# Attention and a gated feed-forward layer on one core: the weights' low parts move to VectorE, four ticks decode twice, and the second unit's input is normalised a tick sooner

## The chip, the core and the metric

The kernel runs on one core of a Trainium2 chip. Its time is the device time of one execution in microseconds (us); lower is better. The engines are PE (TensorE, matrix products), DVE (VectorE), ACT (ScalarE) and POOL (GpSimd), each working through a queue of its own in order; SP (SyncE) issues the loads and stores. PE's granted clock has two levels, 1.2 and 2.4 GHz, shown as a share of the higher one.

## The reference, cut to what matters

Windowed attention over 8 x 8 heads of 576 positions (heads 0 to 3: the last 32 keys; heads 4 to 7: every fourth key of the last 128), then a root-mean-square norm and a gated feed-forward layer on 4608 tokens of width 512, with 1536 hidden columns:

```python
scores = where(mask, q @ k.T / 8, -1e9)
attn = softmax(scores) ; x = attn @ v
xn = x / sqrt(mean(x * x) + 1e-6) * rms_g
g = xn @ w_gate
val = xn @ w_val
out = (g * sigmoid(g) * val) @ w_out
```

The weights reach the kernel as 64-bit numbers.

## The kernel before, in words

The tokens are worked on in 16 units of 288. For each unit the feed-forward layer runs over 12 blocks j of 128 hidden columns in three ticks each: the gate product g, the value product v, and the output product acc of block j - 1. The counter of ticks over the whole main loop is `t` (L793): unit 0 begins at t = 2, unit 1 at t = 36. In the same ticks PE does the attention of the next unit: scores s, transposed probabilities t, outputs o (`products`, L450). Their ticks are a table, `q_at` (L767 for unit 1), that `plan` (L745) turns into events; `plan` also sets when the unit's sum of squares is formed ("sum", PE's rps) and when its norm is applied ("apply", PE's bps, `rms_apply`, L567).

What the other engines do in a tick is put off with `later(dt, rank, fn)` and issued by `flush` (L113) in order of rank. So the order on each engine's queue is fixed by tick and rank. From rank 0 up, a tick issues on DVE the product h of tanh and value (`prod`, L677), the scores' maxima (`scores_max`, L354), the tanh product (`silu`, L664), a decoding step (rank 5) and the low part of a weight (rank 6).

- **Decoding.** The weights come in 18 pairs of 1 MB, `raw`, three buffers. A pair is rescaled by ACT (`rebase`, L151, from pair 3 on), its sign word is cleared by POOL (L162), and DVE puts the number together in two steps from pair 4 on (`rest`, L176, and `whole`, L180; three before that). The step `whole` frees the buffer and issues the next load. `decode(1)` (L797) issues one step per tick in unit 0; the last pair, 17, is whole at t = 32. For the last pair, the rescaling and the clearing are issued right with its first step. Once no more than two steps are left, a second pool of buffers opens (L800), from which unit 1's x gets parts of its space.
- **Splitting.** Unit 0 multiplies with the decoded 32-bit weights. From unit 1 on each weight stands as a high and a low part (`split_weight`, L227): ACT casts the high part, then DVE or POOL subtracts it, which gives the low part lo (L243). The 36 weights are split in the order of their use in unit 0: at even ticks from 4 to 30 on DVE, and from tick 37 on in every tick, on DVE in odd and on POOL in even ones. The line that sets this:

```python
if used and (t >= SPLITS[2] or t % 2 == 0 and SPLITS[0] <= t < SPLITS[1]):
    later(0, 6, lambda: split_weight(*used.pop(0), V if t < SPLITS[1] or t % 2 else G))
```

- **The norm.** PE's rps sums the squares at tick 27; DVE adds the constant, POOL takes the power and splits the root (L537 to L543), a tick later DVE and ACT spread it over a matrix rd (`spread`, L546), and PE's bps multiplies that with ones at tick 30. In the ticks after that DVE scales x (L585) and ACT, DVE and POOL split it.

PSUM has few banks: the gate product of j + 1 takes the bank of the value product of j, and one bank, s, holds every score from tick 4 on.

Of the kernel before, what the change touches and what calls it, by code (L numbers as in the profile page):

```python
# [14 lines left out]
ALU = mybir.AluOpType  # L15
# [22 lines left out]
REBASES = 5, 9, 17, 23  # L38
BUSY = 7, 3
SIGNS = 4  # L40
SPLITS = 4, 31, 37


ORDER = [(0, 0, "q"), (0, 1, "q"), (0, 0, "v"), (0, 2, "q"), (0, 0, "w"), (0, 1, "v"), (0, 3, "qv"), (0, 2, "v"),
         (0, 0, "g"), (0, 0, "w"), (0, 0, "w"), (1, 0, "qv")]
# [22 lines left out]
def attn_moe(ctx: ExitStack, tc: tile.TileContext, qk_in, v_in, w_gate, w_val, w_out, rms_g, outT):  # L68
# [4 lines left out]
    V, A, G, PE = nc.vector, nc.scalar, nc.gpsimd, nc.tensor  # L73
# [36 lines left out]
    def later(dt, rank, fn):  # L110
        put_off.setdefault(now[0] + dt, []).append((rank, fn))

    def flush():  # L113
        for _, fn in sorted(put_off.pop(now[0], []), key=lambda e: e[0]):
            fn()
# [11 lines left out]
    wts, raws, fs, his, los, used = {}, {}, {}, {}, {}, []  # L127
# [74 lines left out]
    def decode(k):  # L202

        for i in range(k):
            later(0, 5 + 2 * i, step)
        later(0, 8.9, rebase_next)
# [16 lines left out]
    def single(kind, j):  # L223
        n = pieces.index((kind, j))
        return fs[n // 2][:, n % 2]

    def split_weight(kind, j, e):  # L227
        n = pieces.index((kind, j))
        m, k = divmod(n, 2)

        tag = f"hi{n if n % 4 == 3 and n < 2 * NP - 4 else n - n % 4}"
        if tag not in his:
            parts = 1 if n % 4 == 3 and n < 2 * NP - 4 else 3 if n < 2 * NP - 4 else 4
            his[tag] = cst.tile([P, parts, NC, P], F32R, tag=tag, name=f"{tag}_{kind}{j}")
        hi = his[tag][:, 0 if tag == f"hi{n}" else n % 4]
        if k == 0:
            los[m] = cst.tile([P, 2, NC, P], F32R, tag=f"slot{state['free']}", name=f"lo_{m}")
        else:
            state["free"] = m
        lo = los[m][:, k]  # L240
        wts[kind, j] = hi, lo
        A.copy(out=hi, in_=single(kind, j))
        e.tensor_tensor(out=lo, in0=single(kind, j), in1=hi, op=ALU.subtract)  # L243


    heads, vs, late = {}, {}, []
# [188 lines left out]
    def bursts(u):  # L435
        return [(u, c, i) for c in range(NC) for i in range(len(geometry(u, c)[0]))]
# [197 lines left out]
    def bank(kind, j):  # L634
        return "gv"[(j + (kind == "v")) % 2]
# [12 lines left out]
    def gate(u, j):  # L648
        g_ps = group("g", u, j)
        if u == 0:  # L650
            used.append(("g", j))
        g = g_ps[:, :U]

        def tanh():
            nonlocal g
            t = (sb.tile([P, U], F32, tag="hhi", name=f"h_{j}", bufs=2) if u == 0 else
                 sb.tile([P, U], F32, tag="th", name=f"th_{u}_{j}", bufs=1))
            if u + j == 0:
                g = sb.tile([P, U], F32, tag="hhi", name="g_first", bufs=2)
                V.tensor_tensor(out=g, in0=g_ps[:, :U], in1=root[0], op=ALU.mult)  # L660
            A.activation(out=t, in_=g, func=AF.Tanh, scale=0.5)  # L661
            gv[u, j] = t

        def silu():  # L664
            t = gv[u, j]
            V.scalar_tensor_tensor(out=t, in0=t, scalar=1.0, in1=g, op0=ALU.add, op1=ALU.mult)  # L666

        later(1, 0 if u + j else 0.65, tanh)
        later(1, 0.8, silu)
        return g_ps[:, U:U + 2 * QB]  # L670

    def val(u, j):
        v_ps = group("v", u, j)
        if u == 0:
            used.append(("v", j))

        def prod():  # L677
            t = gv[u, j]
            V.tensor_tensor(out=t, in0=t, in1=v_ps[:, :U], op=ALU.mult)  # L679
            if u + j == 0:  # L680
                V.tensor_tensor(out=t, in0=t, in1=root[0], op=ALU.mult)

        def parts():
            t = gv.pop((u, j))
            if u == 0:
                hs[u, j] = t
                return
            hi = sb.tile([P, U], F32R, tag="hhi", name=f"hhi_{u}_{j}", bufs=2)
            lo = late[0].tile([P, U], F32R, tag="hlo", name=f"hlo_{u}_{j}", bufs=2)
            A.copy(out=hi, in_=t)  # L690
            G.tensor_tensor(out=lo, in0=t, in1=hi, op=ALU.subtract)  # L691
            hs[u, j] = (hi, lo)

        later(1 if u + j else 2, 0, prod)
        later(1 if u + j else 2, 0.5, parts)
        return v_ps[:, U:U + 2 * QB]

    def proj(u, j):
        if u == 0:
            used.append(("o", j))  # L700
        h = hs.pop((u, j))
        for d in range(NC):
            if j == 0:
                acc[u, d] = ps.tile([P, 512], F32, tag=f"acc{d}", name=f"acc_{u}_{d}")[:, :U]
            three(acc[u, d], weight("o", u, j), d, h, j == 0, j == NJ - 1)
            if j == NJ - 1:
                later(1, 0.7, lambda d=d: give(u, d))
# [35 lines left out]
    events = {}  # L743

    def plan(u, base, q_at, t_at, o_at):  # L745
        for b, *ts in zip(bursts(u), q_at, t_at, o_at):
            for kind, t in zip("qto", ts):
                events.setdefault(base + t, {})[kind] = b
        events.setdefault(base + o_at[-1] + (4 if u == 1 else 3), {})["sum"] = u
        events.setdefault(base + o_at[-1] + (4, 7, 5)[min(u, 2)], {})["apply"] = u  # L750

    def attend(t_ps, **tags):
        e = events.pop(now[0], {})
        if any(k in e for k in "qto"):
            products(e.get("q"), e.get("t"), e.get("o"), t_ps, **tags)
        if "sum" in e:
            rms_sum(e["sum"])
        if "apply" in e:
            rms_apply(e["apply"])

    ends = nb + LAG + OUT + 5
    plan(0, 0, range(nb), range(LAG, nb + LAG), range(LAG + OUT, nb + LAG + OUT))
    for u in range(1, NU):
        q_at = [LAST - (LAST - EARLY[u > NNAT]) * (nb - 1 - k) // (nb - 1) for k in range(nb)]
        t_at, o_at = [t + 5 for t in q_at], [t + 8 for t in q_at]
        if u < NNAT:
            q_at = (-4, -2, -1, 1, 2, 4, 5, 7, 8, 10, 11, 13, 14, 16)  # L767
            t_at, o_at = [t + 5 for t in q_at], [t + 7 for t in q_at]
        plan(u, ends - 2 + 3 * NJ * (u - 1), q_at, t_at, o_at)
    for n in range(ends):  # L770
# [19 lines left out]
    for u in range(NU):  # L790
        for j in range(NJ):
            for part in range(0 if u + j else 2, 3):
                t = 3 * (u * NJ + j) + part  # L793
                if used and (t >= SPLITS[2] or t % 2 == 0 and SPLITS[0] <= t < SPLITS[1]):
                    later(0, 6, lambda: split_weight(*used.pop(0), V if t < SPLITS[1] or t % 2 else G))
                if u == 0:
                    decode(1)  # L797
                opening = len(ops) <= 2
                flush()
                if opening and not late:  # L800
                    early.close()
                    late.append(ctx.enter_context(tc.tile_pool(name="late", bufs=2)))
                if part == 0:
                    free = gate(u, j)
                elif part == 1:
                    free = val(u, j)
                else:
                    if prev is not None:
                        proj(*prev)
                    prev = (u, j)  # L810
                    free = None
                    if "t" in events.get(now[0], {}):
                        free = ps.tile([P, 512], F32, tag=bank("g", j), name=f"t_{u}_{j}")[:, :2 * QB]
                attend(free, s_tag="acc2" if t < 4 else "s")
                now[0] += 1
# [70 lines left out]
```

## Time and profile before

| | us |
|---|---|
| median of 3 runs (1146.93 to 1150.12) | 1148.58 |
| the profiled execution | 1148.22 |
| its span, first to last instruction | 1146.4 |
| PE busy in the span | 1120.8 (98%) |
| DVE busy | 793.4 (69%) |
| ACT busy | 714.6 (62%) |
| POOL busy | 620.8 (54%) |

The chain that ended last lies on PE for 85% of the span and on DVE for 6%. The mean granted clock is 0.997. An engine's busy time is the time in which it executes; what it waits for stands in brackets behind an instruction in the timeline, with the engine and line that ended the wait.

### The profile page before, as it was taken

To read this page: it belongs to the slowest core of one execution; us is meant where nothing else is said; L and a number is where in the kernel's file an instruction comes from. 1 tells how busy PE (TensorE), PEld (TensorE's weight loads), DVE (VectorE), ACT (ScalarE), POOL (GpSimd) and SP (SyncE) were. 2 spreads that over 40 slices of the span, in tenths; PEclk is the share of its full clock that TensorE was granted. 3 is DMA by queue.
4 is the path that set the end of the run, shared out by engine and by line. 5 is a ranking of instruction groups with operands and counts; after the bars stand their busy time and mean duration, and the time that the engine had idled before them with its cause. 6 is when DMAs were issued, how large, how long until landed. Compare 5 with 4: busy or idle time off the path is not lost.

```text
span 1146.4 us, 25956 instructions
## 1 busy us (share of the span) xinstructions
PE 1120.8 (98%) x8357; PEld 1088.0 (95%) x8357; DVE 793.4 (69%) x2893; ACT 714.6 (62%) x2610; POOL 620.8 (54%) x1073
## 2 busy tenths in 40 slices
PE   8898888999999999999999999999999999999998
PEld 7676778999999999999999999999999999999998
DVE  7889865867767586776758677585866758586411
ACT  5686676766657576675757657576765757576311
POOL 8235576655546465564547556465655646565211
PEclk9999999999999999999999999999999999999999
DMA  9555211311212121121212213121221312120000
GB/s 246 168 202 205 89 48 38 93 50 50 83 38 82 40 84 52 52 89 33 79 41 83 58 41 94 34 86 41 71 63 45 95 27 87 41 79 15 2 21 21
DMA packets 61545, 82.19 MB, mean 72 GB/s; under 512 B 7298, under 2 KB 41090, under 8 KB 61410
## 3 DMA queue, kind: packets, MB, share of 16 engines
q1 hardware_dynamic: 61410, 80.54, 23.6%
q8 instruction: 67, 1.10, 0.4%
q14 instruction: 68, 0.56, 0.2%
HBM read 71.08 MB, written 9.44 MB: 70 GB/s over the span
## 4 chain that ended last, share of the span: by engine, by line
PE 85%; DVE 6%; ACT 4%; issue 2%; DMA 1%; POOL 1%; POOLq 0%; SPq 0%; DVEq 0%; ACTq 0%
PE acc L622 8%; PE g L622 8%; PE v L622 8%; PE acc L623 8%; PE g L624 8%; PE g L623 8%; PE acc L624 8%; PE v L623 8%; PE v L624 8%; PE s L489 3%; PE o L477 3%; PE o L478 1%; PE busy L739 1%; ACT t L376 1%; DVE lo L243 1%
## 5 line engine op out<-in xcount | busy, mean ns | idle before, releaser
L691 POOL TENSOR_TENSOR hlo<-th,hhi 128x288 fp32r<-128x288 f32 x180 | 145.2, 807 | 201.5 <-ACT hhi L690 153.7
L624 PE MATMUL acc<-hhi,lo 128*128 128x288 f32 x720 | 212.2, 295 | 0.0
L391 POOL TENSOR_SCALAR t<-t,sum 72x72 f32<-72x72 f32 (+3 forms) x414 | 154.0, 384 | 71.9 <-DVE sum L386 65.2
L624 PE MATMUL v<-xhi,lo 128*128 128x288 f32 x612 | 180.8, 295 | 0.0
L624 PE MATMUL g<-xhi,lo 128*128 128x288 f32 x612 | 180.6, 295 | 0.0
L376 ACT ACTIVATE t<-t,sum 96x128 f32<-96x128 f32 (+3 forms) x448 | 165.6, 375 | 11.7 <-DVE sum L366 11.0
L690 ACT CAST hhi<-th 128x288 fp32r<-128x288 f32 x180 | 78.1, 434 | 141.0 <-DVE th L679 138.8
L305 POOL TENSOR_TENSOR vlo<-vt,vhi 128x128 fp32r<-128x128 f32 x196 | 93.3, 476 | 109.3 <-ACT vhi L301 96.9
L421 DVE TENSOR_TENSOR xraw<-o,xraw 64x96 f32<-64x96 f32 (+1 forms) x392 | 106.8, 272 | 56.4 <-ACT xraw L411 50.4
L661 ACT ACTIVATE th<-g 128x288 f32<-128x288 f32 x180 | 73.9, 410 | 106.6 <-PE g L624 87.7
L624 PEld LDWEIGHTS acc<-hhi,lo 128*128 128x128 f32 x720 | 135.6, 188 | 0.0
L666 DVE SCALAR_TENSOR_TENSOR th<-th,g 128x288 f32<-128x288 f32 x180 | 80.4, 447 | 69.4 <-ACT th L661 69.4
L624 PEld LDWEIGHTS v<-xhi,lo 128*128 128x128 f32 x612 | 115.3, 188 | 0.0
L624 PEld LDWEIGHTS g<-xhi,lo 128*128 128x128 f32 x612 | 115.0, 188 | 0.0
L622 PE MATMUL g<-xhi,hi_g 128*128 128x288 f32 x357 | 110.7, 310 | 1.6 <-DVE sum L385 0.9
L335 POOL TENSOR_TENSOR ks<-qk,ks 128x288 fp32r<-128x288 f32 (+2 forms) x112 | 111.0, 1005 | 0.0
L622 PE MATMUL acc<-hhi,hi_o 128*128 128x288 f32 x360 | 110.8, 308 | 0.0
L411 ACT COPY xraw<-o 64x96 f32<-64x96 f32 (+1 forms) x392 | 101.5, 259 | 12.5 <-PE o L478 10.1
L679 DVE TENSOR_TENSOR th<-th,v 128x288 f32<-128x288 f32 x180 | 81.5, 453 | 38.1 <-PE v L624 30.0
L623 PE MATMUL acc<-hlo,hi_o 128*128 128x288 f32 x360 | 106.9, 297 | 0.0
L361 DVE TENSOR_TENSOR t<-s,mask 96x256 f32<-96x256 f32 (+3 forms) x196 | 71.5, 365 | 50.9 <-PE s L489 45.7
L623 PE MATMUL g<-xlo,hi_g 128*128 128x288 f32 x322 | 94.8, 294 | 0.0
(184 smaller groups left out, 3581.2 us busy)
## 6 DMA issues: line engine op xcount, KB each, us to landing
qk<-in_qk_dram SPq DMA_DIRECT2D x60, 288.0 KB, 2.8
vt<-in_v_dram SPq DMA_DIRECT2D x196, 64.0 KB, 1.9
qk<-in_qk_dram SPq DMA_DIRECT2D x30, 352.0 KB, 3.0
out_dram<-ot SPq DMA_DIRECT2D x64, 144.0 KB, 1.9
qk<-in_qk_dram SPq DMA_DIRECT2D x30, 304.0 KB, 2.8
raw<-in_w_gate_dram SPq DMA_DIRECT2D x12, 512.0 KB, 4.7
raw<-in_w_val_dram SPq DMA_DIRECT2D x12, 512.0 KB, 5.3
raw<-in_w_out_dram SPq DMA_DIRECT2D x12, 512.0 KB, 4.3
```

Of the source, the lines that this page charges most:

```text
L305: G.tensor_tensor(out=vl, in0=vs.pop(b), in1=vh, op=ALU.subtract)
L335: ek.tensor_tensor(out=ks[:, 1, :nkt], in0=kr, in1=ks[:, 0, :nkt], op=ALU.subtract)
L376: A.activation(out=t[:nq, a, :n], in_=t[:nq, a, :n], func=AF.Exp, scale=-1.0, bias=sm[:nq, a, 0:1], accum_out=sm[:nq, a, 1:2] if u else None)
L391: (V if u == 0 and (c, i) > (NC - 1, 0) else G).tensor_scalar(out=t[:nq, a, :n], in0=t[:nq, a, :n], scalar1=sm[:nq, a, 3:4], scalar2=1.0, ...
L411: A.copy(out=to[a * D:(a + 1) * D], in_=o[a * D:(a + 1) * D, (2 + a) * nq:(3 + a) * nq])
L421: V.tensor_tensor(out=to[rows], in0=o[rows, a * nq:(a + 1) * nq], in1=to[rows], op=ALU.add)
L622: PE.matmul(out, wh[:, cc, :], xh, start=start, stop=False)
L623: PE.matmul(out, wh[:, cc, :], xl, start=False, stop=False)
L624: PE.matmul(out, wl[:, cc, :], xh, start=False, stop=stop)
L666: V.scalar_tensor_tensor(out=t, in0=t, scalar=1.0, in1=g, op0=ALU.add, op1=ALU.mult)
L679: V.tensor_tensor(out=t, in0=t, in1=v_ps[:, :U], op=ALU.mult)
L691: G.tensor_tensor(out=lo, in0=t, in1=hi, op=ALU.subtract)
```

## The change

Four things change in the table of ticks, and nothing in the arithmetic.

1. All low parts are DVE's. Splits run at ticks 9 to 30 whose number isn't 2 modulo 3 (15 instead of 14), and from tick 37 on in every tick but each fourth; the last one is at tick 63 instead of 58.
2. Unit 0 issues no decoding step in tick 2 and two in ticks 8, 16, 24 and 28. The last pair is whole at tick 29 instead of 32, and the second pool opens at tick 29 instead of 31.
3. The scores of unit 1 stand one tick later in five places (ticks 6, 9, 12, 15 instead of 5, 8, 11, 14, and 10, 13, 16 as before), with their transposes and outputs.
4. Unit 1's bps stands at tick 29 instead of 30, and its x is scaled and split a tick sooner.

```diff
-SPLITS = 4, 31, 37
+SPLITS = 8, 31, 37
+TWICE = 8, 16, 24, 28
...
-    def split_weight(kind, j, e):
+    def split_weight(kind, j):
...
-        e.tensor_tensor(out=lo, in0=single(kind, j), in1=hi, op=ALU.subtract)
+        V.tensor_tensor(out=lo, in0=single(kind, j), in1=hi, op=ALU.subtract)
...
-        events.setdefault(base + o_at[-1] + (4, 7, 5)[min(u, 2)], {})["apply"] = u
+        events.setdefault(base + o_at[-1] + (4, 6, 5)[min(u, 2)], {})["apply"] = u
...
-            q_at = (-4, -2, -1, 1, 2, 4, 5, 7, 8, 10, 11, 13, 14, 16)
+            q_at = (-4, -2, -1, 1, 2, 4, 6, 7, 9, 10, 12, 13, 15, 16)
...
-                if used and (t >= SPLITS[2] or t % 2 == 0 and SPLITS[0] <= t < SPLITS[1]):
-                    later(0, 6, lambda: split_weight(*used.pop(0), V if t < SPLITS[1] or t % 2 else G))
+                if used and (t % 4 != 0 if t >= SPLITS[2] else t % 3 != 2 and SPLITS[0] <= t < SPLITS[1]):
+                    later(0, 6, lambda: split_weight(*used.pop(0)))
                 if u == 0:
-                    decode(1)
+                    decode(0 if t == 2 else 2 if t in TWICE else 1)
```

The changed kernel is one line longer, so its line numbers behind the table are higher by one: L244 there is L243 here.

DVE's queue around the product h of j = 1 in unit 0 (ticks 3 to 5), before. A name ends in a buffer's number; the numbers ahead of it are unit, chunk and block of an attention tile, or j, or the pair of a weight (f, raw, lo); s is a score, t and sum4 what its maximum writes.

```order
L168 SCALAR_TENSOR_TENSOR f_3_613<-raw_3_392,f_3_613 128x1024
L666 SCALAR_TENSOR_TENSOR h_1_683<-h_1_683,g_0_1_674 128x288
L385 TENSOR_REDUCE sum2_88<-sum2_88 96x2
L386 RECIPROCAL sum2_88<-sum2_88 96x2
L172 SCALAR_TENSOR_TENSOR f_3_613<-raw_3_392,f_3_613 128x1024
L243 TENSOR_TENSOR lo_0_702<-f_0_233,hi0_g0_701 128x512
L679 TENSOR_TENSOR h_1_683<-h_1_683,v_0_1_705 128x288
L366 ISA t_1_1_2_718,sum4_90<-s_1_1_2_710,mask_77 96x128
```

The same place now:

```order
L166 TENSOR_SCALAR f_3_613<-f_3_613 128x1024
L667 SCALAR_TENSOR_TENSOR h_1_679<-h_1_679,g_0_1_670 128x288
L386 TENSOR_REDUCE sum2_88<-sum2_88 96x2
L387 RECIPROCAL sum2_88<-sum2_88 96x2
L169 SCALAR_TENSOR_TENSOR f_3_613<-raw_3_392,f_3_613 128x1024
L680 TENSOR_TENSOR h_1_679<-h_1_679,v_0_1_697 128x288
L367 ISA t_1_1_2_710,sum4_90<-s_1_1_2_702,mask_77 96x128
```

The decoding steps are one further back (the pair's first and second instead of its second and third), and no low part stands ahead of the product and the maximum.

DVE's queue around the product h of j = 9 (ticks 27 to 30), before; rst is the root of unit 1's norm, rd its spread:

```order
L177 SCALAR_TENSOR_TENSOR raw_15_1137<-raw_15_1137 128x1024
L536 TENSOR_SCALAR rst_1_1229<-rps_1_1223 96x3
L666 SCALAR_TENSOR_TENSOR h_9_1227<-h_9_1227,g_0_9_1218 128x288
L181 SCALAR_TENSOR_TENSOR f_15_1196<-f_15_1196,raw_15_1137 128x1024
L243 TENSOR_TENSOR lo_6_1242<-f_6_778,hi12_v4_1241 128x512
L679 TENSOR_TENSOR h_9_1227<-h_9_1227,v_0_9_1245 128x288
L551 TENSOR_TENSOR rd_1_0_1251<-ident_64,rst_hi_1_1232 96x288
L177 SCALAR_TENSOR_TENSOR raw_16_1174<-raw_16_1174 128x1024
```

And now:

```order
L178 SCALAR_TENSOR_TENSOR raw_16_1162<-raw_16_1162 128x1024
L244 TENSOR_TENSOR lo_6_1228<-f_6_794,hi12_v4_1227 128x512
L537 TENSOR_SCALAR rst_1_1242<-rps_1_1236 96x3
L667 SCALAR_TENSOR_TENSOR h_9_1240<-h_9_1240,g_0_9_1231 128x288
L182 SCALAR_TENSOR_TENSOR f_16_1208<-f_16_1208,raw_16_1162 128x1024
L244 TENSOR_TENSOR lo_6_1228<-f_6_794,hi12_v4_1227 128x512
L178 SCALAR_TENSOR_TENSOR raw_17_1219<-raw_17_1219 128x1024
L680 TENSOR_TENSOR h_9_1240<-h_9_1240,v_0_9_1257 128x288
L552 TENSOR_TENSOR rd_1_0_1263<-ident_64,rst_hi_1_1245 96x288
L182 SCALAR_TENSOR_TENSOR f_17_1253<-f_17_1253,raw_17_1219 128x1024
```

Three more decoding steps (two of pair 16, the first of pair 17) and one more low part stand ahead of the product. On POOL the clearing of pair 17's sign word stands right behind the root in both orders.

PE's queue at the end of tick 29, now (before, the bps rows stood behind the gate product g_0_10 and one score):

```order
L620 MATMUL acc_0_2_725<-h_8_1196,f_14_1143 128x288
L620 MATMUL acc_0_3_727<-h_8_1196,f_14_1143 128x288
L572 MATMUL bps_1_1278<-rd_1_0_1263,ones_71 128x288
L572 MATMUL bps_1_1278<-rd_1_1_1265,ones_71 128x288
L620 MATMUL g_0_10_1285<-xn_0_620,f_14_1143 128x288
```

The sum over the root now stands between the output product and the gate product of j = 10.

## Rows read from the trace of the kernel before

**Rows 1.** Busy time by stretch: from:to, length, then each engine's, clock, DMA share, GB/s

```profile
41.75:113.81 72.06, 65.71 (x313) 51.11 (x311) 62.84 (x138) 54.12 (x156) 26.97 (x19) 0.98 0.54 195
113.86:129.79 15.93, 13.76 (x58) 10.18 (x59) 14.57 (x30) 8.42 (x26) 8.48 (x10) 1.00 0.26 91
129.79:189.01 59.22, 49.84 (x356) 47.35 (x357) 42.35 (x159) 43.31 (x152) 41.80 (x63) 0.97 0.21 59
189.01:1146.40 957.39, 953.17 (x7414) 949.19 (x7412) 642.34 (x2428) 583.70 (x2190) 514.26 (x919) 1.00 0.19 56
```

**Rows 2.** PE's timeline in ticks 5 to 6: start, length, line, operation

```profile
51.85 0.58 PE L486 MATMUL s<-qk 128*72 128x104 f32 x4 [2.83 <-DVE sum L366]
52.27 3.81 PE L619 MATMUL g<-xn,f 128*128 128x288 f32 x8
```

**Rows 3.** Busy time by stretch, the two stretches at the lower clock

```profile
148.00:151.40 3.40, 3.40 (x17) 3.38 (x17) 2.02 (x5) 1.87 (x7) 2.99 (x5) 0.51 0.02 5
...
52.30:55.90 3.60, 3.60 (x10) 2.48 (x9) 2.64 (x7) 3.34 (x10) 1.69 (x1) 0.53 0.47 189
```

**Rows 4.** Who PE waited for from 41.75 to 129.7 us

```profile
PE g L619 <- DVE h L679: 3.7, 4, 1.5
```

**Rows 5.** Who PE waited for from 129.7 to 189.01 us

```profile
PE v L622 <- DVE pt L448: 3.3, 2, 1.8
```

**Rows 6.** DVE's timeline ahead of the maximum of tick 5

```profile
50.33 0.69 DVE L243 TENSOR_TENSOR lo<-f,hi_g 128x512 fp32r<-128x512 f32 x1 [0.45 <-ACT hi_g L242]
50.94 0.45 DVE L679 TENSOR_TENSOR h<-h,v 128x288 f32<-128x288 f32 x1
```

**Rows 7.** DVE's decoding steps by line, 40 to 190 us: count, busy us, mean ns

```profile
L177 DVE SCALAR_TENSOR_TENSOR raw<-raw 128x1024 uint32<-128x1024 uint32 x14 | 19.2, 1374 | 0.9 <-POOL raw L162 0.8
L181 DVE SCALAR_TENSOR_TENSOR f<-f,raw 128x1024 uint32<-128x1024 uint32 x14 | 18.6, 1330 | 0.1
```

**Rows 8.** Who DVE waited for from 41.75 to 113.81 us

```profile
DVE lo L243 <- ACT hi_o L242: 3.3, 4, 1.2
DVE lo L243 <- ACT hi_g L242: 2.3, 4, 1.0
```

**Rows 9.** POOL's timeline, the root and the clearing of pair 17

```profile
111.71 1.85 POOL L537 TENSOR_TENSOR rst<-rst,mhalf 96x3 f32<-96x3 f32 x1
...
113.90 1.59 POOL L543 TENSOR_TENSOR rst_lo<-rst,rst_hi 96x3 fp32r<-96x3 f32 x1
118.83 1.15 POOL L162 TENSOR_SCALAR raw<-raw 128x1024 f32<-128x1024 f32 x1 [3.34 <-DVE sum L366]
```

**Rows 10.** PE's timeline in ticks 30 to 36

```profile
113.86 2.21 PE L619 MATMUL g<-xn,f 128*128 128x288 f32 x8 [0.50 <-DVE h L679]
...
116.08 0.81 PE L571 MATMUL bps<-rd,ones 96*128 96x288 f32 x2
116.73 2.11 PE L619 MATMUL v<-xn,f 128*128 128x288 f32 x8
...
129.79 0.37 PE L622 MATMUL g<-xhi,hi_g 128*128 128x288 f32 x1 [0.68 <-ACT pt L446]
```

**Rows 11.** By line, 129.79 to 189.01 us: DVE's q parts, POOL's low parts, ACT's casts

```profile
L344 DVE TENSOR_TENSOR qs<-qk,qs 64x288 fp32r<-64x288 f32 x6 | 5.0, 842 | 0.2
...
L243 POOL TENSOR_TENSOR lo<-f,hi_o 128x512 fp32r<-128x512 f32 x4 | 5.1, 1278 | 0.1
...
L242 ACT CAST hi_o<-f 128x512 fp32r<-128x512 f32 x8 | 4.9, 618 | 0.0
```

**Rows 12.** The q parts: ns min/median/max; then one of them, and POOL beside it

```profile
L344 DVE TENSOR_TENSOR qs<-qk,qs x112: 454/456/1743, 100.9 to 1033.6; 64x288 fp32r<-64x288 f32 x112
...
153.71 1.58 DVE L344 TENSOR_TENSOR qs<-qk,qs 64x288 fp32r<-64x288 f32 x1
...
153.68 1.30 POOL L243 TENSOR_TENSOR lo<-f,hi_g 128x512 fp32r<-128x512 f32 x1
```

**Rows 13.** ACT's timeline, the rescaling of pair 16

```profile
109.30 1.18 ACT L159 ACTIVATE f<-raw 128x1024 f32<-128x1024 f32 x1 [5.33 <-DMA raw<-in_w_val_dram]
```

## The prediction

> **What bounds the kernel now.** I read the stretches first, then the waits of PE (TensorE), then the queues of DVE (VectorE), POOL (GpSimd) and ACT (ScalarE) around each wait. A tick is one step of the main loop: gate (g), value (v) or output (acc) product of one j; ticks are numbered through the whole main loop, unit 0 from tick 2 on and unit 1 from tick 36. From 189.01 us on PE is busy for 953.17 of 957.39 us [rows 1]. The change doesn't touch the steady work behind 189 us, so whatever it does lies before that. There PE loses time in three pieces:
> - Ticks 5 and 6 of unit 0: one wait of 2.83 us for a score's maximum on DVE, and behind it a gate product that took 3.81 us [rows 2], because the granted clock was 0.53 (the 1.2 GHz level) for 3.60 us [rows 3]: 3.60 x 0.47 = 1.7 us lost. Together 4.5 us.
> - Ticks 18 to 35 of unit 0: waits for DVE's product h, 3.7 us in four pieces [rows 4]. A gate product of j + 1 reuses the PSUM bank of the value product of j, so it can't begin before DVE has read that. DVE is the busiest helper: 62.84 of the 72.06 us from 41.75 to 113.81 [rows 1].
> - Ticks 36 to 59, where unit 1 runs with split weights: PE is busy 49.84 of 59.22 us [rows 1], so 9.4 us idle, 3.3 of them for DVE's low part of a transposed tile [rows 5], which waits for ACT's copy; and 3.40 us at a clock of 0.51 [rows 3], another 1.7 us lost.
>
> That is about 20 us that the change could reach at most; it also moves work into the first and second piece.
>
> **1. The start of unit 0 (no decoding step in tick 2, no weight split before tick 9, the score of tick 5 a tick later).** In the old order a decoding step, a low part of 0.69 us with 0.45 us of waiting for ACT ahead of it, and the product at 50.94 stood in front of the maximum for which PE waited [rows 6]. In the new order none of the splits is there, the decoding steps come one tick later, and the next score stands behind the gate product on PE, so PE needs that maximum about 2 us later. I take the whole wait and the half clock behind it: -4.5 us. Bounds: 0 to -4.5.
>
> **2. The rest of unit 0 up to the gate product of j = 10 (tick 30).** Here the change pays. DVE runs in order, and in front of the product h of j = 9 it now also has three decoding steps (two of the pair 16, one of the pair 17) and one more low part: 3 x 1.37 + 0.69 = 4.8 us [rows 6, 7], counting all three steps at the dearer of the two means. So 62.84 + 4.8 = 67.6 us of DVE work lie between 41.75 and that product. DVE's idle time was 72.06 - 62.84 = 9.2 us, of which 5.6 stood before low parts, waiting for ACT's casts [rows 1, 8]. A DVE that is later finds more casts done, so I take 1.5 us for those, 1.9 (about half of the other 3.6) for the rest, and 2 us for a new one: the last pair's first step now stands in front of that product, and on POOL the clearing of the pair's sign word stands behind the root of unit 1's norm. That chain took from 111.71 to 115.49 us, and the clearing 1.15 more [rows 9], 4.9 us from the root's start, while DVE has 0.45 + 1.33 + 0.69 = 2.5 us to do in between (the 0.45 is a product over one tile, by the one at 50.94) [rows 6, 7]. Idle together 5.4 us, and the product ends at 41.75 + 67.6 + 5.4 = 114.8 instead of 113.8. Behind it come DVE's spread of the root (one tile of 96 x 288, which I price like the product of 0.45 us at 50.94) and the sum over it on PE, bps, 0.65 us from 116.08 to the next product [rows 6, 10]: with unit 1's x a tick sooner bps stands ahead of the gate product of j = 10, no longer behind it. That product begins at 115.9, against 113.86 before [rows 10]: +2.0 us net of the 4.5 gained above. Bounds: with 3 us of idle it begins 0.4 us sooner than before, with 8 us 4.6 later.
>
> **3. Ticks 30 to 35.** Before: 15.93 us, with PE idle for 2.2 [rows 1]. Now DVE has no decoding left behind tick 29 and the 0.65 us of bps is gone ahead. I take away the 0.65 and 1.4 of the idle time (the 0.68 before unit 1's first gate product waits for ACT [rows 10] and stays): -2.05. So unit 1 starts at +2.0 - 2.05, the same time as before. Bounds: -2.8 and -0.65.
>
> **4. Ticks 36 to 63 (low parts all on DVE, in three ticks of four).** Before, 11 low parts each ran on DVE and on POOL in ticks 37 to 58. Now DVE has 17 in these ticks and 4 more by tick 63: 6 x 0.69 = 4.1 us more inside the stretch [rows 6]. In return POOL loses 11 of about 1.28 us, 14 us [rows 11]; and ACT's casts, 0.618 us each [rows 11], are spread over 27 ticks, 5 fewer by tick 58: 3.1 us. DVE gets back what POOL's low parts cost it: its q parts took 0.842 us in the mean there, 0.456 as the median of all [rows 11, 12], 6 x 0.39 = 2.3 us. The row behind this is the q part at 153.71, which took 1.58 us with a low part of 1.30 us begun on POOL 0.03 us sooner [rows 12]. The Trainium skill, in "SBUF — State Buffer", section "Who interferes with whom", says that a vector instruction with two SBUF inputs contends with a GpSimd instruction that reads SBUF, and that the one issued first holds the ports while the other fully blocks. By that rule each of POOL's 11 low parts could hold DVE for its whole length, up to 14 us, so the sum could be better than mine by nearly 12; the trace agrees for the pair at 153.7, and a mean of 0.842 says that most did not collide, so I keep 2.3. DVE nets +1.8 us of work and is 42.35 of 59.22 us busy [rows 1], so it is the chains through ACT, not its load, that decide; with 3.1 us less on ACT I take a quarter of the 9.4 us of waits, and lose 0.4 of it again in ticks 59 to 63 where waits had ended: -2.0 us. Bounds: -7 (most waits and the half clock gone) and +4 (17 low parts each make DVE wait for a cast where POOL's did not; a wait of 0.45 us, as ahead of the low part in [rows 6], on ten more of them, is 4.5).
>
> Loads: a pair's buffer is refilled right behind its last step, so pairs are now loaded up to three ticks sooner on the same queue; I cost this at nothing, since ACT, which rescales a pair once it has landed, stood idle for a load for long only once, 5.33 us before 109.30 [rows 13], when it had nothing else to do until PE's next gate product. Where a load comes late now, it is part of the idle time in 2.
>
> **The sum.** 1148.22 us (the profiled execution, span 1146.4) + 2.0 - 2.05 - 2.0 = 1146.2. The median of the runs shown is 0.36 above that execution, so 1146.6 as a median. A measurement of this kernel can tell about 0.3%, 3.4 us, from no change: 1145.1 to 1152.0 count as the same.
>
> **The rivals.**
> - *Gain and payment nearly cancel (forecast, 0.42).* 1146.6, its own range 1145 to 1151. For it: DVE's total work up to unit 1 stays the same but for one low part, and DVE bounds that piece either way.
> - *The waits of unit 1's start clear (0.38).* DVE's casts are ready (3 us of idle in 2: tick 30 at -0.4, unit 1 at -2.5) and POOL's absence with a lighter ACT removes half of the waits behind tick 36 (-5): 1148.6 - 7.5 = 1141. For it: 3.3 us wait for ACT's copy with a cast ahead of it, and long q parts beside POOL. Against it: six low parts more on an in-order DVE. The rule that 4 names from "SBUF — State Buffer" in the Trainium skill would speak for this case.
> - *The norm of unit 1 becomes the wait (slower, 0.20).* The product bps, moved a tick ahead on PE, waits for the root on POOL, and the last pair's step on DVE, queued behind the same root, holds the product h of j = 9. With 8 us of DVE idle, tick 30 begins 4.6 us late; a wait on PE that long is followed by the low clock, as the 2.83 us wait was, 1.7 us more [rows 2, 3]; 2.05 come back by unit 1 and nothing is gained behind it: 1148.6 + 4.6 + 1.7 - 2.05 = 1152.9. For it: root and clearing stand in one POOL queue, 4.9 us [rows 9], and rps on PE is only a value and an output product ahead of bps. It decides once bps begins later than about 117 us.
> - *The last pair isn't whole sooner*, because its load, three ticks sooner, lands no sooner. Then x comes when it did: about 1148, inside the first case's chance.
>
> **How the numbers follow.** Faster by over 0.3% is the second case, 0.38; the same 0.42; slower 0.20. The likeliest case gives 1146.6. For 8 in 10 the range goes down past the second case, to 1139.5, and up to the third, 1153.
>
> **What would show it.** Right: no wait of PE before the score of tick 6 and a full clock at 50 to 56 us; the gate product of j = 10 between 113.5 and 118 with bps just ahead of it, waited for; DVE waiting for POOL before the first step of pair 17; q parts near 0.46 us after 130; PE idle 6 to 8 us in the 59 us behind unit 1's start. Wrong: the first wait replaced by one as long within ten ticks, or DVE so late at tick 37 to 63 that PE's waits there grow past 10 us, or PE free of waits from tick 20 on, which would make the step 2 account too dear.

## The result and the profile after

The changed kernel takes 1153.16 us (median of 7 runs, 1152.54 to 1155.74), the kernel before 1148.16 beside it: ratio 1.0046, interval 1.0034 to 1.0057. It is slower by about 5 us. The profiled execution took 1154.51 us, 1.35 above that median; its span is 1152.7 us, 6.3 more than the one of before.

Where the 6.3 us arise is read from the starts of gate products, counted from the gate product of tick 1 (41.59 us before, 41.66 after):

| gate product of | before | after | after minus before |
|---|---|---|---|
| j = 2 | 10.68 | 8.54 | -2.1 |
| j = 3 | 19.96 | 16.24 | -3.7 |
| j = 5 | 34.89 | 32.89 | -2.0 |
| j = 7 | 50.34 | 50.59 | +0.25 |
| j = 9 | 65.15 | 68.06 | +2.9 |
| j = 10 | 72.27 | 79.08 | +6.8 |
| unit 1, first | 88.20 | 93.88 | +5.7 |
| end of the span | 1104.81 | 1111.04 | +6.2 |

The start gains 3.7 us. By j = 7 they are used up, ticks 21 to 30 lose 6.6, ticks 30 to 35 give 1.1 back, and behind unit 1's start another 0.55 is lost. Busy time by stretch, columns as in [rows 1], with first the kernel before, cut from j = 5 to j = 9:

```profile
76.48:106.74 30.26, 27.18 (x125) 20.68 (x123) 26.86 (x43) 23.19 (x62) 15.42 (x11) 1.00 0.65 229
```

and then the changed kernel, from j = 5 to 9, 9 to 10, 10 to unit 1, and unit 1's first 59.22 us:

```profile
74.55:109.72 35.17, 27.76 (x129) 21.10 (x127) 32.48 (x49) 26.48 (x70) 16.20 (x12) 1.00 0.63 219
109.72:120.74 11.02, 8.63 (x32) 6.52 (x33) 7.88 (x12) 3.38 (x7) 3.35 (x4) 0.85 0.26 96
120.74:135.54 14.80, 14.33 (x58) 10.86 (x57) 9.17 (x27) 5.65 (x21) 5.01 (x8) 0.88 0.09 25
135.54:194.76 59.22, 48.19 (x353) 45.57 (x354) 44.15 (x163) 40.22 (x145) 26.70 (x52) 1.00 0.21 61
```

The third busy column is DVE. From j = 5 to j = 9 it worked 26.86 us before and works 32.48 now; the stretch is 4.9 us longer and DVE fills 92% of it (89% before). From j = 10 on DVE is the least loaded it has been (9.17 of 14.80 us), but PE is then busy for 14.33 of 14.80 us and can't give back more.

PE's timeline of the changed kernel, the rows that waited:

```profile
50.20 2.21 PE L620 MATMUL g<-xn,f 128*128 128x288 f32 x8 [1.10 <-ACT pt L447]
...
74.20 0.51 PE L473 MATMUL o<-pt,v 104*128 104x144 f32 x2 [1.20 <-ACT xraw L409]
...
109.72 3.47 PE L620 MATMUL g<-xn,f 128*128 128x288 f32 x8 [4.14 <-DVE h L680]
...
120.40 0.53 PE L572 MATMUL bps<-rd,ones 96*128 96x288 f32 x2 [2.39 <-DVE rd L552]
...
135.54 0.37 PE L623 MATMUL g<-xhi,hi_g 128*128 128x288 f32 x1 [0.47 <-DMA vt<-in_v_dram]
```

The 2.83 us and the half clock of [rows 2, 3] are gone: the gate product at 50.20 takes 2.21 us. In their place stand 4.14 us ahead of j = 9, with a gate product of 3.47 us behind it, and 2.39 us ahead of bps, with one of 3.79 us behind that (at 120.74 us): the granted clock is 0.85 and 0.88 over those stretches. The lower level comes twice now, as it did before at 52.3 and 148 us [rows 3]; unit 1 is free of it.

DVE between, in the changed kernel (the three low parts), and POOL beside it:

```profile
97.45 1.62 DVE L244 TENSOR_TENSOR lo<-f,hi_g 128x512 fp32r<-128x512 f32 x1
...
102.96 1.61 DVE L244 TENSOR_TENSOR lo<-f,hi_g 128x512 fp32r<-128x512 f32 x1
...
107.73 1.57 DVE L244 TENSOR_TENSOR lo<-f,hi_g 128x512 fp32r<-128x512 f32 x1
```

```profile
97.36 1.17 POOL L163 TENSOR_SCALAR raw<-raw 128x1024 f32<-128x1024 f32 x1 [3.00 <-ACT f L160]
...
101.81 2.21 POOL L163 TENSOR_SCALAR raw<-raw 128x1024 f32<-128x1024 f32 x1 [0.34 <-ACT f L160]
107.41 1.35 POOL L163 TENSOR_SCALAR raw<-raw 128x1024 f32<-128x1024 f32 x1 [3.38 <-ACT f L160]
```

A low part takes 0.69 us alone [rows 6]. Each of these three begins while POOL clears a pair's sign words and ends 0.54 or 0.55 us after POOL does (99.07 against 98.53, 104.57 against 104.02, 109.30 against 108.76). So while POOL's instruction ran, DVE's hardly advanced. The Trainium skill, "SBUF — State Buffer", section "Who interferes with whom", says that a vector instruction with two SBUF inputs contends with a GpSimd instruction that reads SBUF, that the shared ports are an exclusive lock, and that the order of issue decides who blocks; these rows agree.

Whom DVE waited for in the changed kernel from 41.75 to 119.89 us (total, times, longest), to be laid beside [rows 8]:

```profile
DVE raw L178 <- POOL raw L163: 3.8, 3, 2.0
DVE h L667 <- ACT pt L447: 2.4, 4, 1.0
DVE rst L537 <- PE rps L530: 1.1, 1, 1.1
DVE lo L244 <- ACT hi_v L243: 0.7, 1, 0.7
DVE lo L244 <- ACT hi_o L243: 0.7, 2, 0.5
DVE lo L244 <- ACT hi_g L243: 0.2, 1, 0.2
```

The longest of the first kind stands ahead of pair 17's first step, at 118.30 us. What held it is on ACT and then on POOL:

```profile
115.86 1.15 ACT L160 ACTIVATE f<-raw 128x1024 f32<-128x1024 f32 x1 [1.72 <-DMA raw<-in_w_out_dram]
```

```profile
116.41 0.19 POOL L544 TENSOR_TENSOR rst_lo<-rst,rst_hi 96x3 fp32r<-96x3 f32 x1
117.10 1.17 POOL L163 TENSOR_SCALAR raw<-raw 128x1024 f32<-128x1024 f32 x1 [0.49 <-ACT f L160]
```

POOL was at work on the root until 116.60, so the clearing could not have begun sooner; it then waited 0.49 us longer for ACT's rescaling, and that for the pair's load. Pair 17 uses the buffer of pair 15, so its load goes out only when pair 15 is whole (111.24 us), and with the double steps at 24 and 28 its first decoding step comes three ticks sooner.

Unit 1: whom DVE's low parts waited for from 130 to 205 us (casts, and in the kernel before also POOL's vlo), first the kernel before, then the changed one:

```profile
DVE lo L243 <- POOL vlo L305: 2.9, 3, 1.2
DVE lo L243 <- ACT hi_g L242: 1.1, 1, 1.1
DVE lo L243 <- ACT hi_o L242: 0.4, 1, 0.4
```

```profile
DVE lo L244 <- ACT hi_o L243: 4.2, 4, 1.9
DVE lo L244 <- ACT hi_g L243: 2.2, 6, 0.9
DVE lo L244 <- ACT hi_v L243: 2.0, 2, 1.6
```

For casts that is 8.4 us against 1.5. As a whole DVE idles less, though: 15.1 of the 59.22 us behind unit 1's start (59.22 - 44.15) against 16.9 before [rows 1]. PE's two longest kinds of waits there, in the changed kernel from 135 to 215 us, beside [rows 5]:

```profile
PE v L623 <- DVE pt L449: 4.0, 2, 2.3
PE s L490 <- DVE sum L367: 2.9, 3, 1.9
```

The longest of each kind stands right behind a low part that waited for its cast. On DVE:

```profile
142.70 1.03 DVE L244 TENSOR_TENSOR lo<-f,hi_o 128x512 fp32r<-128x512 f32 x1 [1.87 <-ACT hi_o L243]
...
175.32 1.35 DVE L244 TENSOR_TENSOR lo<-f,hi_v 128x512 fp32r<-128x512 f32 x1 [1.63 <-ACT hi_v L243]
```

Behind the first follow, without a pause, two copies of acc and the maximum that PE waits for (it ends at 145.33), behind the second the low part of pt (from 176.70). On PE:

```profile
145.47 0.45 PE L490 MATMUL s<-ks,qs 128*96 128x256 f32 x2 [1.88 <-DVE sum L367]
...
177.06 0.40 PE L623 MATMUL v<-xhi,hi_v 128*128 128x288 f32 x1 [2.28 <-DVE pt L449]
```

### The profile page after: what moved, and what is told of

It is laid out like the page before. It is cut to its first block, busy times and chain, and to the rows that moved or that the text cites. A ratio compares the mean times of both kernels' runs of the same rounds, so it can differ in the third digit from the quotient of the medians.

```text
span 1152.7 us, 25954 instructions
## 1 busy us (share of the span) xinstructions
PE 1121.3 (97%) x8357; PEld 1087.5 (94%) x8357; DVE 798.5 (69%) x2904; ACT 714.1 (62%) x2610; POOL 601.0 (52%) x1062
## 4 chain that ended last, share of the span: by engine, by line
PE 84%; DVE 7%; ACT 4%; issue 2%; DMA 1%; POOL 1%; POOLq 0%; SPq 0%; ACTq 0%; DVEq 0%
PE v L623 8%; PE acc L623 8%; PE g L623 8%; PE acc L624 8%; PE g L624 8%; PE g L625 8%; PE v L624 8%; PE v L625 8%; PE acc L625 8%; PE s L490 3%; PE o L478 3%; PE o L479 1%; PE busy L740 1%; DVE f L182 1%; DVE lo L244 1%
## 5 line engine op out<-in xcount | busy, mean ns | idle before, releaser
L336 POOL TENSOR_TENSOR ks<-qk,ks 128x288 fp32r<-128x288 f32 (+2 forms) x112 | 108.4, 982 | 0.0
```

The lines of the kernel that those rows point to most:

```text
L336: ek.tensor_tensor(out=ks[:, 1, :nkt], in0=kr, in1=ks[:, 0, :nkt], op=ALU.subtract)
```

## The experiments

Each was timed in five rounds beside the kernel before; ratios are to it, with 95% intervals. Some expectations name T1 (four double steps fill VectorE and bring the last pair's load into its own tick), T2 (bps ahead of j = 10's gate product), T3 (low parts on VectorE); the letters of the later ones are explained in the expectation of run 5, 8 or 13.

**1. bps back behind the gate product.** Changed kernel, in the line that sets "apply":

```
-(4, 6, 5)[min(u, 2)]
+(4, 7, 5)[min(u, 2)]
```

> The changed kernel with unit 1's sum over the root (bps) put back one tick later, behind the gate product of j = 10. Theory T1 (four double steps: VectorE carries six more decoding steps ahead of h of j = 9, and the last pair's load, rescale and clear come inside its own tick): the gate product of j = 10 waits for h anyway, so only about 1 us comes back, gate product of j = 10 at 119.5 to 120.5 us, time 1151.5 to 1153. T2 (it is bps ahead of that gate product, waiting for the root, that costs): the gate product begins at 114 to 116 us, the time falls by 4 to 7 us to 1146 to 1149. T3 (low parts all on VectorE): no change from 1153, within 1 us.

Measured: 1152.69 us, 1.0040 (1.0027 to 1.0052). T2 falls. The wait for rd is gone, and the gate product that it delayed now waits for h:

```profile
109.11 3.90 PE L620 MATMUL g<-xn,f 128*128 128x288 f32 x8 [4.14 <-DVE h L680]
...
119.36 2.21 PE L620 MATMUL g<-xn,f 128*128 128x288 f32 x8 [1.94 <-DVE h L680]
```

**2. No double step at 28.** Changed kernel:

```
-TWICE = 8, 16, 24, 28
+TWICE = 8, 16, 24
```

> The changed kernel without the last of the four double steps (ticks 8, 16, 24 only), so that the last pair is whole one tick later and its load has one tick more. T1: VectorE's 2.0 us wait for the clear on POOL and one step of 1.3 us leave the path to h of j = 9: 3 to 4 us, time 1149 to 1150; the 3.5 us wait ahead of the gate product of j = 9 (109.7 us) stays. T2: bps still waits ahead of the gate product of j = 10 for the root; at most 1 us, 1152 to 1153. T3: no change within 1 us.

Measured: 1153.78 us, 1.0047 (1.0034 to 1.0059). (The 3.5 us that the expectation calls a wait are that gate product's length, 3.47; the wait ahead of it is 4.14.) T1's part on the last pair falls: the gate product of j = 10 begins 2.5 us sooner by the table's count (76.56), but the step now waits 2.82 us for its clearing one tick later and j = 11 follows at the lower clock; unit 1 starts at 93.53 against 93.88.

```profile
125.51 0.45 PE L490 MATMUL s<-ks,qs 128*96 128x256 f32 x2 [1.30 <-DVE sum L367]
126.34 3.44 PE L620 MATMUL g<-xn,f 128*128 128x288 f32 x8 [0.38 <-DVE h L680]
```

**3. One double step only.** Changed kernel with TWICE = 8, and bps as in 1.

> The changed kernel with one double step only (tick 8, which gives back the step left out in tick 2), so that decoding from tick 9 on stands where it stood in the kernel before, and bps one tick later as there; low parts, scores and the start as changed. T1: the gain at the start (3.3 to 3.65 us by the trace of the changed kernel) lives on to unit 1 and the waits at 109.7 and 120.7 us go: 1145 to 1147, below both kernels. T2: gate product of j = 10 gains 4 to 7 us against the changed kernel: 1146 to 1149. T3: VectorE's low parts stay, so the loss of ticks 24 to 30 stays: 1151 to 1153.

Measured: 1150.25 us, 1.0016 (1.0007 to 1.0024). None of the three ranges holds it: 2.9 us come back, the largest step of all, but not below the kernel before. In the trace unit 1 starts at 88.54 in the table's count, 0.3 later than before, though j = 3 started 3.7 sooner. The gain of the start is spent between.

**4. Low parts all on VectorE, nothing else.** Kernel before:

```
-split_weight(*used.pop(0), V if t < SPLITS[1] or t % 2 else G)
+split_weight(*used.pop(0), V)
```

> The kernel before with every low part on VectorE, at its old ticks; nothing else changed. T3 (the low parts cost the time): slower by 3 to 5 us, 1151 to 1153. T1 and T2 (the order of decoding or of bps costs it): within 2 us of the kernel before, 1146 to 1150; in its trace the q parts behind 130 us shorten from 0.84 towards 0.46 us.

Measured: 1151.97 us, 1.0031 (1.0020 to 1.0042). T3 holds for itself: 3.6 us from this line alone. Unit 1 starts as before (87.98), and the span behind that start is 4.05 us longer. PE's longest waits there, beside [rows 5]:

```profile
PE v L622 <- DVE pt L448: 4.8, 3, 2.6
PE s L489 <- DVE sum L366: 2.5, 3, 1.9
PE g L622 <- DVE pt L448: 2.1, 3, 0.8
```

The next four take the change apart the other way, each part alone put into the kernel before.

**5. The score ticks.** `q_at`: 5, 8, 11, 14 become 6, 9, 12, 15; these are four places, not the five of the third point of the change.

> The kernel before with only unit 0's score ticks of the change (from the seventh score on: a tick later in four places). Theory Q (they pay at the start and cost nothing later): the 2.8 us wait at 51.9 us and the half clock behind it go, unit 1 starts 2 to 4 us sooner, 1145 to 1147. Theory C (VectorE's and ScalarE's work up to unit 1 is the same sum, so what the start gives is taken back before unit 1): the wait goes, unit 1 starts within 1 us of before, 1148 to 1149.5. Theory X (the new ticks put output products of attention behind ScalarE's rescale): waits for xraw of 1.2 us each at 70 to 92 us as in the changed kernel, 1149 to 1151.

Measured: 1148.09 us, 0.9996 (0.9988 to 1.0005). C: the wait changes its name, not the time. (Of X there is one wait for xraw of 1.3 us; run 7 has only one of 0.3 us, as before.) With the decoding step still in tick 2 the gate product itself waits, and the lower clock follows as before:

```profile
51.18 3.77 PE L619 MATMUL g<-xn,f 128*128 128x288 f32 x8 [2.76 <-ACT pt L446]
```

**6. One decoding step from tick 2 to tick 8.**

```
-decode(1)
+decode(0 if t == 2 else 2 if t == 8 else 1)
```

> The kernel before with only one decoding step moved, from tick 2 to tick 8 (a double step there). Q: the wait at 51.9 us stays, since the score that waits keeps its tick; 1148 to 1149. C: it shortens by up to one step, 1.3 us, and the step is paid at tick 8: 1148 to 1149.5. X: no waits for xraw beyond the 0.3 us of before, 1148 to 1149.

Measured: 1148.36 us, 0.9998 (0.9990 to 1.0007). The profiled execution shows the wait split into 1.78 us at 50.23 and 1.25 at 67.27 with the full clock at both, and unit 1 1.3 us sooner; the median shows nothing of it.

**7. The early low parts.** None before tick 8, then two ticks in three.

> The kernel before with only the early low parts at the ticks of the change (none before tick 8, then two ticks in three, 15 of them by tick 30 instead of 14); the later ones alternate between VectorE and GpSimd as before. Q: as before, 1148 to 1149. C: the start gains 0.7 to 2 us (no low part ahead of the maximum at 51.9 us), the denser ticks 9 to 30 take it back and one low part more is paid: 1148 to 1150. X: the waits for xraw come with these casts and not with the score ticks: three of about 1.2 us at 70 to 92 us, 1149 to 1152.

Measured: 1149.02 us, 1.0004 (0.9995 to 1.0013). C again; PE's waits for h grow to 5.4 us in three, against [rows 4].

**8. The low parts from tick 37 on.** All on VectorE, three ticks in four.

> The kernel before with only the low parts from tick 37 on as changed: all on VectorE, three ticks in four. Theory L (VectorE's 17 low parts in unit 1 cost what the run with all of them on VectorE in every tick showed): 2 to 4 us slower, 1150.5 to 1152.5, nothing different before unit 1, waits for pt of VectorE as long as there (some 5 us). Theory M (three ticks in four is what makes it bearable: the changed kernel lost only about half a us behind unit 1's start): within 1 us, 1148 to 1149.5.

Measured: 1152.59 us, 1.0034 (1.0021 to 1.0046). L, not M. The profiled execution is the fastest of the run's six (1149.95 us). One of its waits is new and lies behind all that the prediction looked at, at unit 2's norm; the last low parts, now later than tick 58, stand ahead of rd and wait for casts:

```profile
204.37 0.51 PE L571 MATMUL bps<-rd,ones 96*128 96x288 f32 x2 [2.44 <-DVE rd L551]
```

```profile
202.02 1.17 DVE L243 TENSOR_TENSOR lo<-f,hi_g 128x512 fp32r<-128x512 f32 x1 [2.43 <-ACT hi_g L242]
```

**9 and 10. The late low parts as before (alternately VectorE and GpSimd, every tick)**, once in run 3, once in the changed kernel:

```
-t % 4 != 0 if t >= SPLITS[2] else t % 3 != 2 and SPLITS[0] <= t < SPLITS[1]
+t >= SPLITS[2] or t % 3 != 2 and SPLITS[0] <= t < SPLITS[1]
...
-split_weight(*used.pop(0))
+split_weight(*used.pop(0), V if t < SPLITS[1] or t % 2 else G)
```

> The run with one double step (tick 8), and its low parts from tick 37 on as in the kernel before: every tick, alternately on VectorE and GpSimd. Theory L (VectorE, in order, stands before each late low part until ScalarE's cast is done, 8 to 9 us in all against under 2 before; that is worth 3 to 4 us): 1146 to 1147.5, VectorE's wait for casts behind 130 us back under 3 us. Theory M (the late low parts cost the changed kernel little, the loss lies in ticks 9 to 30): 1149.5 to 1150.5, as with them on VectorE.

Measured: 1149.16 us, 1.0010 (1.0000 to 1.0020), 1.1 us less than run 3 by the medians, 0.7 by the ratios.

> The changed kernel with all four double steps, and its low parts from tick 37 on as in the kernel before. L: 3 to 4 us back, 1149 to 1150.5; what stays above the kernel before is then the double steps at 16, 24 and 28 and bps ahead of the gate product of j = 10 (T1, T2). M: 1152.5 to 1153.5. The gate products of j = 9 and j = 10 start as late as in the changed kernel by both.

Measured: 1151.28 us, 1.0031 (1.0019 to 1.0042), 1.9 us less than the changed kernel by the medians, 1.7 by the ratios. The direction is L's, the size between L and M: within the change the late low parts cost 1 to 2 us, alone 3.6 to 3.9. The intervals overlap; the spans behind unit 1's start say the same, 1.6 and 1.5 us shorter than in run 3 and in the changed kernel. DVE's waits for casts fall to 3.1 and 2.8 us.

**11 and 12. Low parts of unit 0 on GpSimd**, with the edit of 6: every second one of those before tick 31, then all.

> The kernel before with the decoding step of tick 2 moved to tick 8, and every second one of the low parts before tick 31 on GpSimd instead of VectorE (7 of 14). If VectorE's order and its waits for casts bound unit 0 (L carried over to unit 0): 7 times 0.69 and some 3 us of waiting go from VectorE, less what GpSimd's 1.28 us slow VectorE down beside it: 1144 to 1147. If the two engines shut each other out (a low part on GpSimd holds VectorE as long as it takes): no gain or a loss, 1148 to 1151.

Measured: 1149.70 us, 1.0007 (0.9998 to 1.0015), inside the second reading's range; one wait of 3.32 us for h, ahead of j = 9, with a gate product of 4.21 us behind it.

> The same with all 14 low parts before tick 31 on GpSimd. By the first reading, up to twice the gain: 1141 to 1146, the waits of PE for VectorE's h gone. By the second: 14 times up to 1.28 us of VectorE held, against 14 times 0.69 us and 5.6 us of waits taken from it: 1148 to 1153, and VectorE's decoding steps stretched from 1.23 to 1.8 us and more beside them.

Measured: 1147.80 us, 0.9993 (0.9984 to 1.0001). Neither reading: with all of them the wait at the start falls to 0.56 us, but the gate product of j = 9, which waits for the product h of j = 8, waits 2.55 us, and the lower clock follows:

```profile
104.89 3.86 PE L619 MATMUL g<-xn,f 128*128 128x288 f32 x8 [2.55 <-DVE h L679]
```

What was open by then is which part of the decoding order costs the rest: the double at 24, the double at 28 with the last pair's load, or bps.

**13. Changed kernel with TWICE = 8, 16, 28.**

> The changed kernel without the double step at tick 24 (8, 16 and 28 stay). Theory F (VectorE is full ahead of h of j = 8, so the double at 24 makes the 4.1 us wait ahead of the gate product of j = 9 and the half clock behind it): that wait falls to 2 to 3 us, gate product of j = 9 1.3 to 2 us sooner, and the time falls by 1 to 2 us to 1151 to 1152. Theory P (the last pair's load, rescale and clear, and bps, make the loss whatever stands before): the wait ahead of bps grows by what the first falls, 1152.5 to 1153.5.

Measured: 1151.35 us, 1.0030 (1.0019 to 1.0041): 1.8 less. F. The wait ahead of j = 9 halves:

```profile
107.12 3.24 PE L620 MATMUL g<-xn,f 128*128 128x288 f32 x8 [2.14 <-DVE h L680]
```

**14. TWICE = 8, 16, bps a tick later.**

> Double steps at 8 and 16 only, bps a tick later: one double more than the run with tick 8 alone (1150.25). F: a double at 16 costs a step of 1.3 us ahead of j = 6 and little at unit 1, 1150 to 1151.5. P: as with tick 8 alone, 1150 to 1150.5, since the last pair's load has its tick again.

Measured: 1151.45 us, 1.0029 (1.0017 to 1.0040): the same as 13, which still has the double at 28 and bps ahead.

**15. TWICE = 8, 16, 24, bps a tick later.**

> Double steps at 8, 16 and 24, bps a tick later: neither of the two parts that P names. P: both together give back what each alone did not, 1150 to 1151. F: the double at 24 and its wait ahead of j = 9 stay, 1151.5 to 1152.5.

Measured: 1153.17 us, 1.0046 (1.0032 to 1.0059), above the 1151.5 to 1152.5 that F expected and far from P. Without both of the parts that P names the time is that of the changed kernel, and the wait ahead of j = 9 is whole again:

```profile
109.87 3.31 PE L620 MATMUL g<-xn,f 128*128 128x288 f32 x8 [4.12 <-DVE h L680]
```

So doubles at 8; 8 and 16; 8, 16 and 24 give 1.0016, 1.0029, 1.0046 (3, 14, 15), and adding 28 together with bps to the last two of these changes nothing (13, and the changed kernel). Neighbours among the three have overlapping intervals; the first and the last don't. Two pairs differ by the double at 24 alone, the changed kernel and 13, and 15 and 14: 1.8 and 1.7 us by the medians, with the wait ahead of j = 9 twice as long in both (4.14 against 2.14, 4.12 against 2.21). The four kernels with all low parts as changed and a double at 24 (the changed one, 1, 2, 15) lie between 1.0040 and 1.0047, the two without it but with one at 16 at 1.0029 and 1.0030.

Where in the execution this arises, the traces don't settle. One execution each, counted as in the table of the result:

| | unit 1 starts | span behind that start |
|---|---|---|
| before | 88.20 | 1016.6 |
| changed | 93.88 | 1017.2 |
| 1 | 91.15 | 1018.3 |
| 2 | 93.53 | 1018.5 |
| 3 | 88.54 | 1018.9 |
| 13 | 90.62 | 1018.0 |
| 14 | 89.71 | 1018.8 |
| 15 | 90.58 | 1019.0 |

Runs 1, 13 and 15 start unit 1 some 3 us sooner than the changed kernel and lose 0.8 to 1.8 us of it again behind that start. Runs 13 and 15 start it at the same count, though their medians are 1.8 us apart: 1.1 of that lie behind the start, and 0.8 ahead of the gate product of tick 1 (41.04 and 41.80 us), where the two kernels don't differ.

**16. A version that beats both.** Edit of 6, and:

```
-V if t < SPLITS[1] or t % 2 else G
+G if t < 20 else V if t < SPLITS[1] or t % 2 else G
```

> A try to beat both: the kernel before with the decoding step of tick 2 moved to tick 8 and the low parts before tick 20 on GpSimd, those of ticks 20 to 30 on VectorE as before. With all 14 on GpSimd the gate product of j = 8 waited 2.55 us for h, behind a clear and a low part of 1.5 us each on GpSimd at 99 to 103 us. If that queue on GpSimd made the wait: it falls to 1.5 us as before and the half clock goes, 1145 to 1147. If VectorE's sum makes it, 1147.5 to 1149.

Measured: 1146.90 us, 0.9988 (0.9979 to 0.9997): faster than the kernel before by 1.4 us, a little, with an interval that just leaves out no change, and than the changed one by some 6. The expectation's first case holds: the wait ahead of j = 9 (the one that it calls j = 8) falls from 2.55 to 1.64 us, and the clock stays at its upper level there; ahead of j = 8 stands one of 0.79.

```profile
96.59 2.21 PE L619 MATMUL g<-xn,f 128*128 128x288 f32 x8 [0.79 <-DVE h L679]
104.32 2.21 PE L619 MATMUL g<-xn,f 128*128 128x288 f32 x8 [1.64 <-DVE h L679]
```

## Why the prediction was wrong

The forecast, 1146.6, lies 6.6 us below the median measured; its range ended at 1153.0, just short of it. By steps:

- **Step 1** was right in its mechanism and in most of its size: 3.7 us by j = 3 where 4.5 was taken; a wait of 1.10 us for ACT stayed at 50.20. Runs 5 to 7 add what the trace of before didn't tell: none of its three parts alone moves the median.
- **Step 2 is the one that failed in size**, +2.0 against +6.8. Its sum can be laid beside the trace term by term. DVE's work up to the product h was taken as 67.6 us and came to 68.26, the stretched low parts among it. Idle, the term that was mis-sized, was taken as 5.4 us and came to 78.14 - 68.26 = 9.9. The waits for casts were right (1.5 taken, 1.6 measured), and so was the new wait ahead of pair 17's first step (2 taken, 2.0 measured). The rest was taken as half of what it had been, 1.9 us, without a reason for the half, and came to about 6: two more waits for POOL's clearing (1.8), for ACT's copy of pt (2.4), for PE's rps (1.1). A wait that goes was taken as time won, but a queue that runs further ahead meets the next thing that is late. The high bound, 8 us of idle and 4.6 late, was too low as well.
- **Step 3**: -2.05 taken, -1.13 measured. PE's idle time did go, from 2.2 to 0.5 us, but 1.8 us went to the lower clock (0.88 over 14.80 us), which the step left out.
- **Step 4 had the wrong sign**: -2.0 taken, +0.55 in the trace, +1.1 and +1.9 by runs 9 and 10, and 3.6 to 3.9 in runs 4 and 8. DVE's work was sized exactly: +1.8 us taken, 42.35 to 44.15 measured. The q parts did shorten as taken, from 0.842 us [rows 11] to 0.512 (by line, 130 to 190 us of the changed kernel: count, busy us, mean ns):

```profile
L345 DVE TENSOR_TENSOR qs<-qk,qs 64x288 fp32r<-64x288 f32 x8 | 4.1, 512 | 0.2
```

What the step put down only as its bad bound came: low parts on DVE that wait for casts, 8.4 us in all against 1.5, with the maxima and copies behind them. For PE's two longest waits (1.88 and 2.28 us) the rows show this; that it makes up the whole cost is argued, for DVE's idle time as a whole fell at the same time (16.9 to 15.1 us). The trace's +0.55 is small by luck: PE's idle time in the 59.22 us behind unit 1's start rose from 9.4 to 11.0 us, past the 10 us that the prediction named as a sign of being wrong, but this execution had no lower clock there (1.00 against 0.97 before). Between run 3 and run 9, and between the changed kernel and run 10, that clock is the same (0.94 twice, 1.00 twice), and the spans behind unit 1's start differ by 1.6 and 1.5 us. ACT's casts being spread wider didn't help (run 8 against run 4, 1.0034 and 1.0031). By the rule of the Trainium skill that step 4 weighed ("SBUF — State Buffer", section "Who interferes with whom"), up to 12 us more were to be won from the same removal, by an estimate of the prediction. The q parts say that DVE was held less, but the time did not follow.
- **Loads at nothing**: wrong by trace, without a price of its own. Pair 17's load did come late (1.72 us of waiting on ACT at 115.86), yet run 2, which gives it another tick, is no faster.
- **The third rival** gave 1152.9, and its signs came: bps at 120.40, past the 117 us named, waiting for rd, and the lower clock behind it. Its mechanism is at most a part of the cause, and that the time fits is luck. The first step of pair 17 did wait behind the root, which held POOL until 116.60, but 0.49 us more by way of its load, and 2.0 us in all, the clearing included, as step 2 had taken. Without bps ahead, without the double at 28, or without both (runs 1, 2 and 15) the median stays at 1152.7 to 1153.8, although unit 1 starts 2.7 and 3.3 us sooner in the traces of runs 1 and 15 than in the changed kernel's; what the two parts cost by themselves stays open. What costs by the medians is a tick sooner: the double at 24 fills DVE ahead of the product h on which the gate product of j = 9 waits (1.8 us in run 13, 1.7 in run 14 against 15), and, not clear of noise, the one at 16 before it.

The account by ratios, in us: from the changed kernel to run 10 the late low parts, 1.7; from there to run 9 the double steps at 16 to 28 with bps, 2.4; from there to the kernel before the start and the early low parts, 1.1, in an interval that begins at no change. Together 5.3. Taken in the other order, over run 3, the double steps come to 3.4 and the late low parts to 0.7: the two costs are not independent, and why was not tried. That the start's gain is lost between j = 3 and j = 7 is shown by the table; that ACT's rescaling ahead of its copies for the waits on xraw (three of 1.0 to 1.2 us, at 74.20 us the first) is its cause was not tried alone.

## What to carry to other kernels

Work moved sooner on a helper engine pays only where that engine has room; where it is full, a step that is moved ahead can delay the main engine by its own length or more (here 1.2 us for the double at 16, though not clear of noise, and 1.7 to 1.8 for the one at 24, by the medians), and the main engine can give back later no more than its own idle time there (here 2.2 us). Before an operation that waits for another engine is moved to an in-order queue, count what stands behind it there: its wait is paid as well as its duration. And a rival whose time fits has still to be tried by taking its own parts away.

## What was not expected of the hardware

The end of a low part on DVE followed the end of POOL's clearing by 0.54 or 0.55 us three times in three, so here a collision could be timed from POOL's row alone. It goes both ways: the clearing at 101.81 us, which began together with a decoding step on DVE, took 2.21 us, where the one at 97.36 took 1.17. After a wait of 2.14 us the gate product of j = 9 ran at the lower clock (3.24 us, run 13), after one of 2.21 us in run 14 and one of 2.73 us in run 7 it did not (2.21 us both): the length of the one wait ahead doesn't tell which, and the lower clock, which made the gate products behind such waits 1.0 to 2.0 us longer (3.24 to 4.21 us), can't be put into a sum as certain. The rows of run 14 and run 7:

```profile
107.18 2.21 PE L620 MATMUL g<-xn,f 128*128 128x288 f32 x8 [2.21 <-DVE h L680]
...
108.00 2.21 PE L619 MATMUL g<-xn,f 128*128 128x288 f32 x8 [2.73 <-DVE h L679]
```
